# A fused attention, soft-MoE and FFN kernel: dispatch softmax by token tile, a ninth weight tile beside the streamed ones, and another order at the beginning

## The chip, the cores and the metric

The kernel runs on one core of one Trainium2 chip. The metric is the device time of one execution in microseconds (us). PE is TensorE (PEld its weight loads), DVE is VectorE, ACT is ScalarE, POOL is GpSimd, and SP issues most DMAs.

## The reference, cut to what matters

```python
# attention: B, H, S, D = 4, 8, 768, 64, a few global keys and a local window
scores = 0.125 * q @ k.T + bias             # masked
x = softmax(scores, -1) @ v                 # -> (3072 tokens, 512)
# soft MoE: 8 experts, 4 slots each = 32 slots
logits = x @ phi                            # (3072, 32)
d = exp(logits - logits.max(0)); d /= d.sum(0) + 1e-9   # dispatch: softmax over the tokens
slot_input = d.T @ x                        # (32, 512)
slot_out[e] = relu(slot_input[e] @ w1[e]) @ w2[e]       # w1 512x1024, w2 1024x512, float32
c = softmax(logits, 1); x = c @ slot_out    # combine: softmax over the slots
# second FFN
out = relu(x @ w_in) ** 2 @ w_out
```

## The kernel before, in words

Every engine has a queue of its own, and the kernel writes the order of all queues by hand; semaphores only make an engine wait. Three stages follow each other.

**Attention, to 184 us.** The work is 48 units (4 batches, 3 pairs of token tiles, 4 pairs of heads), two to an iteration of the loop at L538. A unit's steps are `stage_qk` (PE, scores `s`, L224), `stage_max` (DVE, mask and row maximum, L238), `stage_exp` (ACT, L257), `stage_T` (PE, transposes into `pt`, L268), `stage_ev` (copies to `pT`, L274, one on DVE and one on ACT), `stage_pv` (PE, `o`, L285) and `stage_x` (ACT, `xT`). Before the loop stands a hand-written beginning, with dummy matmuls (`warm`, L81) between the first steps, and the eight masks are built by DVE, ACT (mask 1, L159) and POOL (masks 2 to 7, L161).

Four units finish a chunk of 256 tokens, 12 chunks in all. A chunk goes through `route(k)`, a generator that is run in small steps (`step(n)`) between the stages of later units. Its front makes the logits: `lt` (L354), `pl` (L364), then on DVE `rc`, two products `lh` (L387) and a sum into `c_tok` (L343), then `px` (L333) and `xb` (L336). An odd chunk ends there; an even chunk goes on with its back, for itself and the odd chunk before (T = 4 token tiles of 128). The back is an online softmax over tokens with the 32 slots held four times over 128 partitions: POOL copies each logit four times (`l`, L391), PE transposes T blocks of 128x128 into `pq` (L406), DVE takes the maximum (L425), ACT the exponential (L427) and the correction factor `fo` (L428), PE transposes T blocks back into `pd` (L437), and `pS` (L455) adds to the running sum `acc`, each group of 32 partitions for another token tile, all with one maximum `nm`. Temporary PSUM tiles share four banks (tag "m"), so a transpose also waits until an earlier tile in its bank was read.

**Experts, 184 to 236 us.** 16 weight tiles of 2 MB (`w1_e`, `w2_e`) pass through SBUF. `NPRE` = 8 of them, the `w1`, have places of their own (`p0` to `p7`) and are loaded in 32 quarters during the loop. Three more places (`s0` to `s2`) come free with the attention's memory. All further loads go into places whose tile is used up, in the order of `items` with the places of `SLOTS` (L189), and the first FFN weights (`win_0`, `wout_0`, 1 MB each) stand ahead of `w2_7`, which comes in four parts. PE multiplies `w1` (L648, 16 matmuls a tile) and `w2` (L740). In program order DVE does `spread` (L717), then `conv_in(0)` and most of `conv_out(0)` (L750, L751, L754: the raw words of the FFN weights made float32), then the copy `soT` (L911), on which the FFN's first matmuls rest.

**FFN, 236 us to the end.** Two chained matmuls over five slices of the hidden width; nothing of it is changed but the places of two tiles.

Of the kernel before, what the change touches and what calls it, by code (L numbers as in the profile page):

```python
# [20 lines left out]
P = 128  # L21
# [7 lines left out]
EPS = 1e-9  # L29
NPRE = 8  # L30
TB = 256
WIDTHS = [256, 384, 512, 512, 384]
NBLK = NT // TB

C_ID, C_SI, C_SI4, C_R2, C_J = 0, 128, 160, 288, 416
C_W = 544
W_REL = S + (QT - 1) * P
# [3 lines left out]
def attention_moe_ffn(ctx: ExitStack, tc, qk, vx, nn, phi, w1, w2, w_in, w_out, consts, relw, out):  # L41
# [11 lines left out]
    ident = con[:, C_ID : C_ID + P]  # L53
    si = con[:, C_SI : C_SI + NS]
    si4 = con[:, C_SI4 : C_SI4 + P]
    n_i = full("n_i", [1, 4], I32)
    n_1 = full("n_1", [1, 4])
    n_f = full("n_f", [P, 4])
    phi_s = full("phi_s", [P, NPR, NS])
    phib = full("phib", [P, NPR, 2, NS])  # L60
# [74 lines left out]
    V.tensor_copy(n_1, n_i)  # L135
    warm(8, zero, idle)
    n_p = aps.tile([P, 512], F32, tag="m", name="n_p", bufs=4)
# [50 lines left out]
    wt = {}  # L188
    SLOTS = [f"p{i}" for i in range(NPRE)] + ["s0", "s1", "s2"] + [f"p{i}" for i in (0, 1, 4, 5, 6, 6, 7)]  # L189

# [123 lines left out]
    fronts = []  # L314

    def route(k, tail=False, back=True):
        xT = xTs[k]
        lg = c_tok[:, 2 * k : 2 * k + 2, :]
# [26 lines left out]
        if tail:  # L345
            ph = pl.rearrange("p (t h s) -> p t h s", h=H, s=NS)
            products(pl, range(2))
            yield
        else:
            pt = [bank(f"lt{k}_{hh}") for hh in range(2)]  # L350
            for pr in range(NPR):
                for hh in range(2):
                    r = slice(hh * D, hh * D + D)
                    nc.tensor.matmul(pt[hh][pr * NS : pr * NS + NS, 0:TB], lhsT=phi_s[r, pr, :], rhs=xT[r, pr, :], start=True, stop=True)  # L354
            yield
            lt = post.tile([P, 2, TB], F32, tag="lh", name=f"lt{k}")
# [14 lines left out]
        if tail:  # L371
            l5 = post.tile([P, 2, 5, NS], F32, tag="l5", name=f"l5{k}")
            scaled(lh[:, :, 0:4, :], 0, 4)
            added(l5[:, :, 0, :], lh[:, :, 0:4, :])
            xTs.pop(k)
            pl = bank(f"pl{k}_2")
            ph = pl.rearrange("p (t h s) -> p t h s", h=H, s=NS)
            products(pl, range(2, 4))
            yield
            scaled(l5[:, :, 1:5, :], 4, 8)  # L380
            added(lg, l5)
            yield
            turn(0, range(NPR))
            yield
        else:
            for t in range(2):
                V.tensor_tensor(lh[:, t].rearrange("p (h g) s -> p h g s", g=2), ph[:, t],  # L387
                                rc[:, t].rearrange("p (h g) -> p h g", g=2).unsqueeze(3).broadcast_to([P, NPR, 2, NS]), op=ALU.mult)
            added(lg, lh)
            l2 = post.tile([P, 2, 4, NS], F32, tag="l5", name=f"l2{k}") if back else att.tile([P, 2, 4, NS], F32, tag="l2", name=f"l2{k}", bufs=1)  # L390
            G.tensor_copy(l2, lg.unsqueeze(2).broadcast_to([P, 2, 4, NS]))  # L391
            for t in range(2):
                px.append(bank(f"px{k}_{t}"))
                turn(t, range(NPR))
                yield
                rows(t)
# [6 lines left out]
        pq = bank(f"pq{k}", tail)  # L403
        for t in range(T):
            if not tail:
                nc.tensor.transpose(pq[:, t * P : t * P + P], parts[t // 2][0][:, t % 2, :, :].rearrange("p a s -> p (a s)"), ident)  # L406
                continue
            for g in range(4):
                nc.tensor.matmul(pq[g * NS : g * NS + NS, t * P : t * P + P], lhsT=lg[:, t, :], rhs=ident, start=True, stop=True)
# [96 lines left out]
    for i in range(2):  # L506
# [13 lines left out]
        stage_max(i + 2, 1)  # L520
        if i == 1:

            G.memset(phib, 0.0)
            for hh in range(2):
                G.tensor_copy(phib[hh * D : hh * D + D, :, hh, :], phi_s[hh * D : hh * D + D, :, :])
        load_qk(i + 6)
# [517 lines left out]
def layout(inputs):  # L1044
# [34 lines left out]
    con[i, C_ID + i] = 1  # L1079
    con[i, C_SI + i % NS] = 1  # L1080
# [36 lines left out]
```

## Time and profile before

| | us |
|---|---|
| three runs | 539.74, 540.13, 541.6 (median 540.13) |
| the profiled execution, its own time | 541.12 |
| its span, first to last instruction | 539.2 |
| PE busy | 523.6 |
| DVE busy | 393.7 |
| ACT busy | 309.9 |
| POOL busy | 174.9 |

The span is 1.9 us shorter than the execution's own time. A busy share is an average over the three stages; what an engine limits is seen in a stage's own rows, in the idle time before an instruction (in brackets, with what ended it) and in the waits.

### The profile page before, as it was taken

The numbers are of one execution on the slowest core, as the hardware profiler recorded it, in microseconds if no ns is written. First come the engines' busy times: TensorE is split into PE (matmuls) and PEld (weight loads), VectorE is DVE, ScalarE is ACT, GpSimd is POOL, SyncE is SP. The second block draws the span as 40 slices with busy tenths as digits, with TensorE's granted clock in tenths as the row PEclk, the third lists the DMA queues.
The fourth block names the chain that finished last, engine by engine and source line by source line (L and its number), as shares of the span: only waits on it lengthen the run. The fifth ranks groups of instructions, "written<-read, shape, count | busy, mean of one in ns | idle before, by whom it ended". The sixth has DMA issues, their size and how long they took to land.

```text
span 539.2 us, 10211 instructions
## 1 busy us (share of the span) xinstructions
PE 523.6 (97%) x3659; PEld 394.9 (73%) x3659; DVE 393.7 (73%) x984; ACT 309.9 (57%) x813; POOL 174.9 (32%) x160
## 2 busy tenths in 40 slices
PE   8999999999999899899999999999999999999997
PEld 5786677777767734256778788878888878888885
DVE  5888879798888764558869897978857757545553
ACT  4987887878786511255775655545544445434441
POOL 7100000000000010024664576455554437544441
PEclk9999999999999999999999999999999999999999
DMA  8889999899962499953041304030030000003333
GB/s 263 271 265 325 322 321 303 312 330 313 325 200 79 161 422 424 416 221 131 27 157 19 139 1 157 0 118 0 1 117 1 0 2 1 0 2 117 118 117 117
DMA packets 25545, 89.13 MB, mean 165 GB/s; under 512 B 2834, under 2 KB 3474, under 8 KB 23314
## 3 DMA queue, kind: packets, MB, share of 16 engines
q1 hardware_dynamic: 25344, 88.30, 45.5%
q8 instruction: 30, 0.49, 0.4%
q14 instruction: 25, 0.20, 0.1%
q10 hardware_dynamic: 146, 0.13, 0.1%
HBM read 82.13 MB, written 6.29 MB: 164 GB/s over the span
## 4 chain that ended last, share of the span: by engine, by line
PE 74%; DVE 12%; DMA 6%; ACT 5%; issue 1%; POOL 1%; DVEq 0%; ACTq 0%; POOLq 0%
PE acc L859 14%; PE acc L860 14%; PE acc L861 14%; PE s L224 6%; PE pt L268 6%; DMA w<-in_w 6%; PE o L285 5%; PE h L841 3%; ACT sm L257 2%; DVE sm L238 2%; PE lt L354 1%; PE px L333 1%; DVE cvyi L751 1%; PE idle L81 1%; DVE rg L846 1%
## 5 line engine op out<-in xcount | busy, mean ns | idle before, releaser
L849 POOL TENSOR_TENSOR g<-rg,g 128x512 fp32r<-128x512 f32 (+1 forms) x109 | 136.8, 1257 | 166.1 <-DVE rg L846 163.4
L859 PE MATMUL acc<-w,g 128*128 128x512 f32 x384 | 151.8, 395 | 1.0 <-DVE oacc L865 1.0
L861 PE MATMUL acc<-w,g 128*128 128x512 f32 x384 | 150.2, 391 | 0.7 <-POOL g L849 0.7
L860 PE MATMUL acc<-w,g 128*128 128x512 f32 x384 | 150.7, 392 | 0.0
L845 ACT ACTIVATE rg<-h 128x512 f32<-128x512 f32 (+1 forms) x109 | 59.7, 548 | 122.0 <-PE h L841 110.8
L867 DVE TENSOR_TENSOR oacc<-acc,oacc 128x512 f32<-128x512 f32 x95 | 65.3, 687 | 58.3 <-PE acc L861 58.3
L257 ACT ACTIVATE sm<-sm,nm 128x256 f32<-128x256 f32 (+1 forms) x192 | 92.7, 486 | 12.3 <-DVE nm L244 10.9
L861 PEld LDWEIGHTS acc<-w,g 128*128 128x128 f32 x384 | 72.1, 188 | 18.6 <-POOL g L849 3.0
L859 PEld LDWEIGHTS acc<-w,g 128*128 128x128 f32 x384 | 72.1, 188 | 17.8 <-DVE oacc L865 1.8
L860 PEld LDWEIGHTS acc<-w,g 128*128 128x128 f32 x384 | 72.4, 189 | 11.1
L846 DVE SCALAR_TENSOR_TENSOR rg<-h,rg 128x512 f32<-128x512 f32 (+1 forms) x109 | 67.7, 621 | 17.1 <-ACT rg L845 17.1
L238 DVE CUSTOM_DVE_ANT_0 sm<-s,mask 128x256 f32<-128x256 f32 (+1 forms) x192 | 67.3, 396 | 4.0 <-PE s L224 3.1
L848 ACT ACTIVATE g<-rg 128x512 fp32r<-128x512 f32 (+1 forms) x109 | 63.4, 581 | 3.5
L391 POOL COPY l<-c_tok 128x256 f32<-128x256 f32 x11 | 4.4, 402 | 162.2 <-DVE c_tok L343 133.8
L224 PE MATMUL s<-raw 64*128 64x256 f32 (+1 forms) x384 | 52.6, 394 | 0.0
L268 PE MATMUL pt<-con,sm 128*128 128x128 f32 x352 | 46.4, 278 | 1.4 <-DVE xb L336 1.4
L285 PEld LDWEIGHTS o<-pT,v 128*64 128x64 f32 x704 | 37.9, 137 | 9.9 <-ACT pT L274 5.2
L285 PE MATMUL o<-pT,v 128*64 128x128 f32 x704 | 44.2, 276 | 0.5 <-issue 0.2
L268 PEld LDWEIGHTS pt<-con,sm 128*128 128x128 f32 x352 | 38.2, 141 | 7.8 <-DVE xb L336 2.9
L841 PEld LDWEIGHTS h<-cu 128*128 128x128 f32 x192 | 35.9, 188 | 7.3
L224 PEld LDWEIGHTS s<-raw 64*128 64x128 f32 x384 | 31.2, 191 | 12.5 <-issue 8.5
L841 PE MATMUL h<-cu 128*128 128x256 f32 x192 | 39.9, 280 | 0.0
(157 smaller groups left out, 567.9 us busy)
## 6 DMA issues: line engine op xcount, KB each, us to landing
raw<-in_qk SPq DMA_DIRECT2D x48, 384.0 KB, 5.6
w<-in_w SPq DMA_DIRECT2D x36, 512.0 KB, 6.8
w<-in_w SPq DMA_DIRECT2D x7, 2048.0 KB, 12.0
v<-in_vx SPq DMA_DIRECT2D x48, 256.0 KB, 4.2
out_x<-oacc SPq DMA_DIRECT2D x23, 256.0 KB, 2.0
win<-in_w_in SPq DMA_DIRECT2D x2, 2048.0 KB, 8.6
wout<-in_w_out SPq DMA_DIRECT2D x2, 2048.0 KB, 8.4
win<-in_w_in SPq DMA_DIRECT2D x2, 1536.0 KB, 10.4
```

The lines of the kernel that those rows point to most:

```text
L224: nc.tensor.matmul(sc[hh][:, tt, 0:n, :], lhsT=r[r0 : r0 + D, tt, :], rhs=rhs, start=True, stop=True)
L238: V.tensor_tensor_reduce(out=sm[:, j, 0:n, :], in0=sc[hh][:, tt, 0:n, :], in1=m[:, 2:3, :] if n == 1 else m[:, 0:2, :], scale=1.0, scalar= ...
L257: nc.scalar.activation(sm[:, j, 0:n, :], sm[:, j, 0:n, :], AF.Exp, bias=nm[:, j : j + 1], scale=QK_SCALE, accum_out=chunk_sums(i // NPR)[: ...
L268: nc.tensor.transpose(pp[tt][:, hh, c, :], sm[:, 2 * tt + hh, c, :], ident)
L285: nc.tensor.matmul(o[hh * D : hh * D + D, tt, :], lhsT=v[:, tt + 2 * c, hh * D : hh * D + D], rhs=pT[:, 2 * tt + hh, c, :], start=c == 0, ...
L841: nc.tensor.matmul(ph[:, k, :], lhsT=U[:, c0 : c0 + P], rhs=cst[:, n * TB : n * TB + TB], start=True, stop=True)
L846: V.scalar_tensor_tensor(g, ph[:, k0:k1, :], 0.0, r, op0=ALU.max, op1=ALU.mult)
L849: G.tensor_tensor(g2[:, 1, js, :], g, g2[:, 0, js, :].bitcast(F32), op=ALU.subtract)
L859: nc.tensor.matmul(pa, lhsT=ghi[:, j, ms], rhs=whi[:, j, :], start=j == 0, stop=False)
L860: nc.tensor.matmul(pa, lhsT=ghi[:, j, ms], rhs=wlo[:, j, :], start=False, stop=False)
L861: nc.tensor.matmul(pa, lhsT=glo[:, j, ms], rhs=whi[:, j, :], start=False, stop=j == J - 1)
L867: V.tensor_tensor(o, pa, o, op=ALU.add)
```

## The change

1. Chunks 0 to 8 (`UNITED` = 8) run the back's softmax apart for each token tile: the logits of up to four tiles are transposed at once, 128 tokens by up to 4 x 32 columns, so that each group of 32 partitions is one token tile with a maximum, a sum and a factor of its own. POOL's fourfold copy falls away, and one `yield` with it. After chunk 8, `unite()` takes the minimum of the four `nm`, rescales `rden` and `acc`, and adds up `rden` over the groups. Chunks 9 to 11 go as before.
2. `NPRE` is 9: `w2_0` gets a place `p8` and is loaded by four more quarters in two later iterations. `SLOTS` has one entry less behind the three streamed places. Room comes from constants (`si` is a part of `si4`, `phi_s` and its GpSimd copies into `phib` fall away, since the host lays out `phib`), from `soT` in a later pool and from a smaller reserved region for dynamic DMAs.
3. At the beginning a small Exp stands on ACT ahead of mask 1, so that its function table is loaded there, and `stage_qk(1)` follows `stage_qk(0)` with no dummy matmuls between; ten dummies instead of eight stand first, and six fall away.

```diff
-NPRE = 8
+NPRE = 9
-C_ID, C_SI, C_SI4, C_R2, C_J = 0, 128, 160, 288, 416
+C_ID, C_SI4, C_R2, C_J = 0, 128, 256, 384
-    phi_s = full("phi_s", [P, NPR, NS])
-    soT = full("soT", [P, 4, NS])
     nc.scalar.dma_start(n_i, nn)
+    nc.scalar.activation(rm[:, 0:1], zero[:, 0:1], AF.Exp)
-    warm(8, zero, idle)
+    warm(10, zero, idle)
-    SLOTS = [f"p{i}" for i in range(NPRE)] + ["s0", "s1", "s2"] + [f"p{i}" for i in (0, 1, 4, 5, 6, 6, 7)]
+    SLOTS = [f"p{i}" for i in range(NPRE)] + ["s0", "s1", "s2"] + [f"p{i}" for i in (0, 1, 4, 5, 5, 6)]
+    UNITED = 8
+    def unite():
+        old = run["nm"]
+        pn = bank("pn")
+        nc.tensor.transpose(pn[0:1, 0:P], old, ident)
+        m1 = post.tile([1, 4, NS], F32, tag="db", name="m1")
+        V.tensor_reduce(m1, pn[0:1, 0:P].rearrange("p (g s) -> p s g", s=NS).unsqueeze(1).broadcast_to([1, 4, NS, 4]), axis=AX.X, op=ALU.min)
+        yield
+        pm = bank("pm")
+        nc.tensor.matmul(pm[:, 0:1], lhsT=m1.rearrange("p g s -> p (g s)"), rhs=si[0:1, 0:1], start=True, stop=True)
...
+        V.tensor_copy(nm, pm[:, 0:1])
+        fo = post.tile([P, 1], F32, tag="fo", name="fou")
+        nc.scalar.activation(fo, old, AF.Exp, bias=nm, scale=-1.0)
+        V.tensor_tensor(rden, rden, fo, op=ALU.mult)
+        yield
+        pr = bank("pr")
+        nc.tensor.matmul(pr[:, 0:1], lhsT=si4, rhs=rden, start=True, stop=True)
+        V.tensor_copy(rden, pr[:, 0:1])
+        G.tensor_scalar(acc, acc, fo, None, op0=ALU.mult)
     def route(k, tail=False, back=True):
+        apart = k <= UNITED
...
-            l2 = post.tile([P, 2, 4, NS], F32, tag="l5", name=f"l2{k}") if back else att.tile([P, 2, 4, NS], F32, tag="l2", name=f"l2{k}", bufs=1)
-            G.tensor_copy(l2, lg.unsqueeze(2).broadcast_to([P, 2, 4, NS]))
+            l2 = None
+            if not apart:
...
+        R = slice(0, T * NS if apart else P)
+        C = P if apart else T * P
+        if apart:
+            nc.tensor.transpose(pq[R, 0:P], c_tok[:, 2 * k + 2 - T : 2 * k + 2, :].rearrange("p t s -> p (t s)"), ident)
+        for t in range(0 if apart else T):
...
-        V.tensor_reduce(mx[R], pq[R, 0 : T * P], axis=AX.X, op=ALU.max)
+        V.tensor_reduce(mx[R], pq[R, 0:C], axis=AX.X, op=ALU.max)
...
             yield
-            yield
+            if not apart:
+                yield
         pd = bank(f"pd{k}")
-        for t in range(T):
+        if apart:
+            nc.tensor.transpose(pd[:, R], dT[R, 0:P], ident[R, R])
+        for t in range(0 if apart else T):
...
+            if k == UNITED:
+                yield from unite()
...
-                    nc.tensor.matmul(pt[hh][pr * NS : pr * NS + NS, 0:TB], lhsT=phi_s[r, pr, :], rhs=xT[r, pr, :], start=True, stop=True)
+                    nc.tensor.matmul(pt[hh][pr * NS : pr * NS + NS, 0:TB], lhsT=phib[r, pr, hh, :], rhs=xT[r, pr, :], start=True, stop=True)
-    warm(6, zero, idle)
     stage_qk(0)
-    nc.sync.dma_start(phi_s, phi)
+    stage_qk(1)
+    nc.sync.dma_start(phib, phi)
...
     warm(5, zero, idle)
-    stage_qk(1)
     stage_max(0, 0)
```

In PE's queue, at the back of chunk 6 (its `pq` starts at 123.97 us in the trace of before), stand before the change `pq`, `stage_pv` of two units, `stage_qk` of one, and `pd`:

```order
L406 MATMUL pq_2019<-con,l_1782 128x128 x2
L406 MATMUL pq_2019<-con,l_1958 128x128 x2
L285 MATMUL o_2024<-pT_1981,v_1831 64x128 x8
L285 MATMUL o_2033<-pT_1992,v_1833 64x128 x8
L224 MATMUL s_0_2059<-raw_1941 128x256
L224 MATMUL s_1_2060<-raw_1941 128x256
L224 MATMUL s_0_2059<-raw_1941 128x256
L224 MATMUL s_1_2060<-raw_1941 128x256
L437 MATMUL pd_2079<-con,dT_2049 128x32 x4
L268 MATMUL pt_0_2084<-con,sm_1926 128x128 x4
```

and after it:

```order
L432 MATMUL pq_1984<-con,c_tok 128x128
L284 MATMUL o_1986<-pT_1946,v_1799 64x128 x8
L284 MATMUL o_1995<-pT_1957,v_1801 64x128 x8
L223 MATMUL s_0_2021<-raw_1908 128x256
L223 MATMUL s_1_2022<-raw_1908 128x256
L223 MATMUL s_0_2021<-raw_1908 128x256
L223 MATMUL s_1_2022<-raw_1908 128x256
L468 MATMUL pd_2041<-con,dT_2011 128x128
L267 MATMUL pt_0_2046<-con,sm_1893 128x128 x4
```

`pq` and `pd` are one transpose each instead of four, at the same places; `pS` comes one step earlier (ahead of the next unit's scores), and so does the whole front of the odd chunk that follows.

In DVE's queue, at the front of chunk 7, an odd one (the row ahead of these is the last row maximum of a unit; `pl` and `px` are PSUM tiles of PE), stand before:

```order
L244 TENSOR_SCALAR nm_2232<-mx_2231 128x4
L368 TENSOR_SCALAR rc_2161<-sums_1757 128x16
L369 RECIPROCAL rc_2161<-rc_2161 128x16
L387 TENSOR_TENSOR lh_2256<-pl_2202,rc_2161 128x256 x2
L343 TENSOR_REDUCE c_tok<-lh_2256 128x64
L336 TENSOR_TENSOR xb_2162<-px_0_2262,rc_2161 128x512
```

and after the change:

```order
L243 TENSOR_SCALAR nm_2137<-mx_2136 128x4
L391 TENSOR_SCALAR rc_2098<-sums_1737 128x16
L392 RECIPROCAL rc_2098<-rc_2098 128x16
L410 TENSOR_TENSOR lh_2168<-pl_2161,rc_2098 128x256 x2
L366 TENSOR_REDUCE c_tok<-lh_2168 128x64
L273 COPY pT_2187<-pt_0_2177 128x512
```

The products and their sum now stand ahead of the next iteration's copy `pT`, where before they stood behind that iteration's copies and maxima; `xb` of both tiles follows later, in one place.

SP's queue, from the loads of unit 45 on to the start of the experts (`w_7` is `w1_7`; of before, `w_0` to `w_2` are `w2_0` to `w2_2`):

```order
L103 DMA raw_2532<-in_qk 128x768
L103 DMA raw_2534<-in_qk 128x768
L109 DMA v_2536<-in_vx 128x512
L109 DMA v_2538<-in_vx 128x512
L103 DMA raw_2649<-in_qk 128x768
L109 DMA v_2651<-in_vx 128x512
L109 DMA v_2653<-in_vx 128x512
L109 DMA v_2765<-in_vx 128x512
L109 DMA v_2767<-in_vx 128x512
L205 DMA w_0_2978<-in_w 128x4096
L205 DMA w_1_2980<-in_w 128x4096
L205 DMA w_2_2982<-in_w 128x4096
```

and after the change (`w_0` is `w2_0`, now in quarters; `w_1` on are `w2_1` on):

```order
L204 DMA w_0_2380<-in_w 128x1024 x2
L102 DMA raw_2487<-in_qk 128x768
L102 DMA raw_2489<-in_qk 128x768
L108 DMA v_2491<-in_vx 128x512
L108 DMA v_2493<-in_vx 128x512
L204 DMA w_0_2380<-in_w 128x1024 x2
L102 DMA raw_2602<-in_qk 128x768
L108 DMA v_2604<-in_vx 128x512
L108 DMA v_2606<-in_vx 128x512
L108 DMA v_2728<-in_vx 128x512
L108 DMA v_2730<-in_vx 128x512
L204 DMA w_1_2947<-in_w 128x4096
```

Two pairs of quarters have come in between the last loads of the attention, and one load of 2 MB less remains behind it.

## Rows read from the trace of the kernel before

**Rows 1.** Chain that ended last, 184 to 240 us: start, us, what.
```profile
198.01 12.89 DMA w<-in_w
...
210.92 19.85 DMA w<-in_w
...
230.81 1.05 PE pSO L740 x4
...
233.67 0.30 DVE soT L911
```

**Rows 2.** DMA view, 180 to 235 us: throughput in 40 equal slices.
```profile
GB/s 0 0 214 334 465 405 429 405 453 417 447 405 453 375 453 393 399 441 441 405 411 441 441 417 405 441 441 411 393 417 405 426 390 405 417 432 429 429 429 429
```

**Rows 3.** Timeline, 184 to 240 us: start, us, engine, line, [idle before].
```profile
220.52 5.36 PE L740 MATMUL pSO<-w,hZ 128*32 128x512 f32 x48
220.81 1.04 DVE L717 TENSOR_TENSOR cu<-pc,cu 64x384 fp32r<-64x384 f32 x2 [1.62 <-ACT cu L716]
...
223.22 0.43 DVE L750 TENSOR_SCALAR cvyi<-raw 128x512 int32<-128x512 int32 x1 [1.37 <-DMA raw<-in_w_in]
...
231.43 0.69 DVE L754 SCALAR_TENSOR_TENSOR cvyo<-cvxo,cvyo 128x512 int32<-128x512 int32 x1
...
233.67 0.29 DVE L911 COPY soT<-pst 128x128 f32<-128x128 f32 x1 [1.55 <-PE pst L910]
```

**Rows 4.** Windows: stretch, its us, busy us of PE, PEld, DVE, ACT, POOL.
```profile
66.59:82.00 15.41, 15.00 (x166) 11.05 (x162) 11.64 (x44) 12.76 (x46) 0.03 (x1) 1.00 0.92 318
...
110.78:126.94 16.16, 15.90 (x166) 12.13 (x166) 15.55 (x60) 11.87 (x43) 0.81 (x2) 1.00 0.93 323
...
148.00:162.50 14.50, 14.07 (x136) 10.41 (x137) 12.53 (x49) 11.86 (x43) 0.40 (x1) 1.00 0.61 191
```

**Rows 5.** Waits, 16 to 184 us: engine, line, whom, total us, times, longest.
```profile
PEld pt L268 <- DVE xb L336: 2.9, 7, 0.8
...
PE pd L437 <- ACT dT L427: 1.4, 4, 0.4
PE pt L268 <- DVE xb L336: 1.4, 4, 0.6
```

**Rows 6.** Timeline of PE, 118 to 150 us.
```profile
123.97 0.66 PE L406 MATMUL pq<-con,l 128*128 128x128 f32 x4
124.55 1.97 PE L285 MATMUL o<-pT,v 128*64 128x128 f32 x32
...
127.78 0.43 PE L437 MATMUL pd<-con,dT 32*128 32x32 f32 x4 [0.19 <-ACT dT L427]
128.14 1.97 PE L268 MATMUL pt<-con,sm 128*128 128x128 f32 x16
...
143.90 0.66 PE L268 MATMUL pt<-con,sm 128*128 128x128 f32 x4 [0.26 <-DVE xb L336]
```

**Rows 7.** Timeline of DVE, 118 to 150 us.
```profile
124.94 0.68 DVE L425 TENSOR_REDUCE rmax<-pq 128x1 f32<-128x512 f32 x1
```

**Rows 8.** Timeline, 0 to 16 us.
```profile
5.58 1.65 PE L224 MATMUL s<-raw 64*128 64x128 f32 x8
...
5.86 1.28 ACT L159 ACT_TABLE_LOAD   x1 [5.86 <-DVE mtmp L147]
...
6.11 7.24 POOL L161 TENSOR_SCALAR mask<-mtmp 128x384 bf16<-128x384 f32 x6
...
7.27 0.29 DVE L238 CUSTOM_DVE_ANT_0 sm<-s,mask 128x128 f32<-128x128 f32 x1 [0.85 <-PE s L224]
...
10.48 0.93 PE L224 MATMUL s<-raw 64*128 64x128 f32 x8
...
12.24 0.59 ACT L274 COPY pT<-pt 128x512 f32<-128x512 f32 x1 [0.44 <-PE pt L268]
```

**Rows 9.** Windows, as rows 4; the granted clock follows POOL.
```profile
4.00:5.60 1.60, 1.60 (x10) 0.92 (x9) 1.20 (x5) 0.00 (x0) 0.96 (x3) 1.00 1.00 293
...
15.00:20.00 5.00, 5.00 (x48) 3.62 (x44) 4.14 (x23) 5.00 (x20) 0.07 (x2) 1.00 0.97 318
```

More of the change, by code (lines that the diff above doesn't have):

```diff
@@ L33 @@
 NBLK = NT // TB
-C_ID, C_SI, C_SI4, C_R2, C_J = 0, 128, 160, 288, 416
-C_W = 544
+C_ID, C_SI4, C_R2, C_J = 0, 128, 256, 384
+C_W = 512
 W_REL = S + (QT - 1) * P
@@ L53, in attention_moe_ffn @@
     ident = con[:, C_ID : C_ID + P]
-    si = con[:, C_SI : C_SI + NS]
     si4 = con[:, C_SI4 : C_SI4 + P]
+    si = si4[:, 0:NS]
     n_i = full("n_i", [1, 4], I32)
@@ L314, in attention_moe_ffn @@
     fronts = []
+    UNITED = 8
[8 more added lines that the diff above has]
+        nc.tensor.matmul(pm[:, 0:1], lhsT=m1.rearrange("p g s -> p (g s)"), rhs=si[0:1, 0:1], start=True, stop=True)
+        nm = post.tile([P, 1], F32, tag="nmr", name="nmu", bufs=2)
+        run["nm"] = nm
+        V.tensor_copy(nm, pm[:, 0:1])
[7 more added lines that the diff above has]
+        G.tensor_scalar(acc, acc, fo, None, op0=ALU.mult)
     def route(k, tail=False, back=True):
+        apart = k <= UNITED
         xT = xTs[k]
@@ L389, in route @@
             added(lg, lh)
-            l2 = post.tile([P, 2, 4, NS], F32, tag="l5", name=f"l2{k}") if back else att.tile([P, 2, 4, NS], F32, tag="l2", name=f"l2{k}", bufs=1)
-            G.tensor_copy(l2, lg.unsqueeze(2).broadcast_to([P, 2, 4, NS]))
+            l2 = None
+            if not apart:
+                l2 = post.tile([P, 2, 4, NS], F32, tag="l5", name=f"l2{k}") if back else att.tile([P, 2, 4, NS], F32, tag="l2", name=f"l2{k}", bufs=1)
+                G.tensor_copy(l2, lg.unsqueeze(2).broadcast_to([P, 2, 4, NS]))
             for t in range(2):
@@ L415, in route @@
         yield
-        R = slice(0, P)
         old = run["nm"]
@@ L424, in route @@
         dT = post.tile([P, 2 * TB], F32, tag="dT", name=f"dT{k}")
-        V.tensor_reduce(mx[R], pq[R, 0 : T * P], axis=AX.X, op=ALU.max)
+        V.tensor_reduce(mx[R], pq[R, 0:C], axis=AX.X, op=ALU.max)
         V.scalar_tensor_tensor(nm[R], mx[R], -1.0, old[R], op0=ALU.mult, op1=ALU.min)
-        nc.scalar.activation(dT[R, 0 : T * P], pq[R, 0 : T * P], AF.Exp, bias=nm[R], scale=1.0, accum_out=dn[R])
+        if apart and T == 2:
+            V.tensor_copy(nm[2 * NS : P], old[2 * NS : P])
+        nc.scalar.activation(dT[R, 0:C], pq[R, 0:C], AF.Exp, bias=nm[R], scale=1.0, accum_out=dn[R])
         nc.scalar.activation(fo[R], old[R], AF.Exp, bias=nm[R], scale=-1.0)
@@ L433, in route @@
             yield
-            yield
+            if not apart:
+                yield
         pd = bank(f"pd{k}")
-        for t in range(T):
+        if apart:
+            nc.tensor.transpose(pd[:, R], dT[R, 0:P], ident[R, R])
+        for t in range(0 if apart else T):
             nc.tensor.transpose(pd[:, t * NS : t * NS + NS], dT[0:NS, t * P : t * P + P], ident[0:NS, 0:NS])
@@ L472, in route @@
             V.scalar_tensor_tensor(acc[A], acc[A], fo[A], pS[A], op0=ALU.mult, op1=ALU.add)
-            if T == 2 and k:
+            if T == 2 and not apart:
                 A = slice(2 * NS, P)
                 V.tensor_scalar(acc[A], acc[A], fo[A], None, op0=ALU.mult)
+            if k == UNITED:
+                yield from unite()
     queue = []
@@ L520, in attention_moe_ffn @@
         stage_max(i + 2, 1)
[L521 to L525, printed above, removed]
         load_qk(i + 6)
@@ L692, in attention_moe_ffn @@
         G.memset(odd[r0 : r0 + NS], -1.0)
+    soT = ex.tile([P, 4, NS], F32, tag="soT", name="soT")
     crs = {}
@@ L1079, in layout @@
     con[i, C_ID + i] = 1
-    con[i, C_SI + i % NS] = 1
     for g in range(4):
@@ L1085, in layout @@
     relw = (i[:, None] - np.arange(W_REL)[None, :] + (QT - 1) * P).astype(np.float32)
+    phi = pm(inputs["moe_phi"], 4)
+    phib = np.zeros((P, 4, 2, NS), phi.dtype)
+    for hh in range(2):
+        phib[hh * D : hh * D + D, :, hh, :] = phi[hh * D : hh * D + D].reshape(D, 4, NS)
     w1, w2 = inputs["moe_w1"], inputs["moe_w2"]
@@ L1090, in layout @@
         "nn": words([np.asarray(inputs[n], np.int64) for n in ("n_local", "n_global")]).reshape(1, 2).view(np.int32),
-        "phi": pm(inputs["moe_phi"], 4),
+        "phi": phib,
         "w1": np.ascontiguousarray(w1.reshape(E, 4, P, F).transpose(0, 2, 1, 3)),
@@ L1103 @@
     from concourse.bass_utils import run_bass_kernel_spmd
-    nc = bacc.Bacc("TRN2", target_bir_lowering=False, num_devices=1)
+    nc = bacc.Bacc("TRN2", target_bir_lowering=False, num_devices=1, dynamic_dma_scratch_size=1024)
     lay = layout(inputs)
```

## The prediction

> **What bounds the kernel now.** I read the chain of work that ended last first, because it shows which stage is held by something else than PE. It names PE nearly everywhere, but between 198.01 and 230.77 us two pieces of a DMA of weights hold it [rows 1]. The DMA view of that stretch says why: from about 185 us on it moves 375 to 465 GB/s in every slice without a gap [rows 2]. So the experts' stage is as long as its 18 MB take (eight tiles of `w2` and two of 1 MB), and the last 2 MB tile, which comes in four parts, decides: PE has finished the tile before at 225.88 (220.52 and 5.36), but the matmuls of the fourth part start only when it has landed, at 230.81, and end at 231.86 (1.05 more) [rows 1, 3].
>
> The attention is different. Its windows (after the stretch: length, busy time with the count of instructions of each engine, granted clock, DMA share, GB/s) show PE busy 15.90 of 16.16 us where an even chunk's back runs, and 15.00 of 15.41 where an odd front runs [rows 4]. PE's only waits of size there are 1.4 us for the exponential ahead of `pd` and 1.4 us for DVE's `xb` ahead of a transpose, whose weight loads wait 2.9 us [rows 5]. So PE time that is saved in an even back should be gained, as long as DVE, busy 15.55 of the 16.16 us, follows.
>
> In the beginning DVE's first maximum waits for PE's scores, at 7.27 us, and the masks are late too: ACT's table load starts only at 5.86 and takes 1.28 us ahead of mask 1 [rows 8].
>
> **The change part by part.** *Ninth tile, loads.* `w2_0` (2.097 million bytes) leaves the full stretch. At 430 GB/s, the middle of rows 2, that is 4.9 us: every later load lands 4.9 us sooner. Its four quarters go into two later iterations. The stretch 148.0 to 162.5 moves 191 GB/s at a share of 0.61, and 2.1 MB in 14.5 us more are 145 GB/s, together 336, beside 318 and 323 in the stretches before [rows 4]. The only queue that they pass is SP's, whose next loads wait for PE anyway; I take nothing for it. Without that cover two quarters would delay the next scores' data by 2.4 us (1.05 MB at 430 GB/s).
>
> *What is late next.* PE would finish the last tile at 225.88 and a third of 5.36 (16 of 48 matmuls, 1.79), 227.67 instead of 231.86: 4.2 us. But the copy `soT` at 233.67 stands on DVE behind the conversion, which began at 223.22 because the raw words landed then, and ended at 232.12 (231.43 and 0.69), 8.90 us later [rows 3]. With the words 4.9 us sooner it begins when DVE is done with `spread`, at 221.85 (220.81 and 1.04), and ends at 230.75. `soT` then stands there, 2.9 us sooner, not 4.2. I take **-2.9**, bounds -1.4 (only the conversion's shift) and -4.2.
>
> *Even backs.* Four transposes of `pq` hold PE from 123.97 to 124.55, 0.145 each, four of `pd` from 127.78 to 128.14 [rows 6]. One each remains: 0.58 + 0.36 - 2 x 0.145 = 0.65, in four backs with T = 4 (chunks 2, 4, 6, 8) 2.6, and 0.2 in chunk 0 with T = 2. The wait ahead of `pd` (1.4 in four) goes as well: the maximum over 512 columns takes 0.68 [rows 7], over 128 an estimate of a quarter to a half of that, and the exponential shrinks too, while `pd` keeps its place behind the same PE work. Together **-4.2**; bounds 0, if another engine binds, and -4.2. The copies of POOL hide beside others and are worth nothing alone.
>
> *Odd fronts.* One `yield` less brings each odd front forward by a step. DVE forms `lh` and `c_tok` in a gap where it waited for transposes, and `xb` is done before the transposes that need its bank. The 1.4 us that PE waited for `xb` go: **-1.4**. Upper bound the 2.9 of the weight loads, lower nothing: the copy `pT` is now behind those products, and `stage_pv` waits for it.
>
> *`unite`.* Three small transposes or matmuls on PE, at most 0.145 each: **+0.4**. Worse could be DVE: its copy of `nm` waits for `pm`, which stands on PE behind two units of `stage_pv` (1.97 from first to last [rows 6]). Behind that copy on DVE wait the next unit's maxima, then its exponential, then its transposes, an iteration later. PE has those two units, scores and four transposes queued meanwhile, so I charge no more; the bound is +2.
>
> *Beginning.* With the table loaded early, mask 1 no longer waits 1.28 us, and with no dummies between, both units' scores are done sooner. The first maximum can start when mask 0 is there, about 0.7 us before 7.27. Behind the copy at 12.24 ACT is the engine without a gap (5.00 of 5.00 us from 15 to 20 [rows 9]), so what it starts earlier is what the stage gains: **-0.7**, bounds 0 and -1.3. More is not to be had, since POOL's last mask ends at 13.35 (6.11 and 7.24) [rows 8].
>
> Sum: -2.9 - 4.2 - 1.4 + 0.4 - 0.7 = -8.8. The profiled execution took 541.12 us, so 532.3; the median of the runs, 540.13, lies 1.0 below that execution, so **531.3**. The FFN stage only shifts.
>
> **The rivals.** *DVE takes over in the attention* (0.20). For it: 15.55 of 16.16 us busy in an even back [rows 4], and in `unite` it stands still. Then an even back gains only what DVE sheds, an estimated 0.4 (0.68 less a good third) each, 1.6, odd fronts nothing, and `unite` costs its 2: the attention loses 0.4; with 0.7 and 2.9 the gain is 3.2: 536.9. Against it: in the odd stretch DVE has 3.8 us free of 15.41.
>
> *The experts' stage does not gain* (0.07): the ninth tile is resident, but a load waits for its place, or the conversion holds the same time. The sum without 2.9 is 5.9: 534.2.
>
> *More is gained* (0.10): 4.2 in the experts (1.3 more), 2.9 in the odd fronts (1.5 more), 1.3 at the beginning (0.6 more). All three make 12.2 and 527.9, two of them about 10.9 and 529.
>
> *Nothing measurable* (0.03): the attention goes as in the first rival (0.4 lost), and the conversion does not move; of the beginning's 0.7 then 0.3 remains, 539.8.
>
> *Slower, by PE's clock at the beginning* (0.03). [...]
>
> **How the numbers follow.** The forecast has 0.57, its own range 529.5 to 533.5 (odd fronts and `unite` at either bound). From 528.0 to 537.0 the first three rivals are in; nothing and slower lie out, and what the others spill over: about 0.1. Within 0.3% (1.6 us) a measurement of this kernel can't tell a change from none. Faster by more: 0.57 + 0.20 + 0.07 + 0.10 = 0.94, of which I take 0.01 away for mishaps; same 0.03; slower 0.04.
>
> **What the profile of the changed kernel would show.** The chain should hold PE, ACT or DVE at `soT`, no longer a DMA up to it, and the conversion should begin right behind `spread`. `pq` and `pd` should be one matmul each, with no wait for the exponential, and the wait of transposes for `xb` be gone. About 5 us should lie between the old and the new end of the attention (184 us), of them 0.7 by the copy that stood at 12.24. Around `unite` DVE should show an idle time of 1 to 2 us for `pm` that PE does not follow. I am wrong if PE waits for DVE's `pT` in odd chunks or for `pm` and `pr`, if scores wait for their data near 150 us, or if the conversion is later than DVE allows.

## The result, and the profile after

The changed kernel takes 532.16 us (median of four runs, 532.12 to 532.35) against 540.42 for the kernel before (539.74 to 541.6): a ratio of 0.9846, with a 95% interval from 0.9828 to 0.9864. The profiled execution took 532.15 us with a span of 530.1. Three positions divide the gain of 9.1 us in the span: the copy `slotZ`, which ends the attention, moved from 193.97 to 188.16 (5.81); from there to the copy `soT` it is 36.85 us instead of 39.70 (2.85); what follows took 0.44 less.

The chain of work that ended last, 176 to 240 us (start, us, what), holds no DMA any more up to `soT`, where [rows 1] had 32.74 us of it:

```profile
206.03 5.29 PE pSO L770 x48
...
216.07 0.44 DVE cvyi L780
...
224.28 0.69 DVE cvyo L784
225.01 0.30 DVE soT L941
```

The conversion begins right behind `spread`, without a wait, and `soT` follows its last operation at once: from 215.01 to 225.30 DVE pauses for 0.68 us only, for ACT. In the attention, the windows over the same two stretches of iterations as the first two of [rows 4] (columns as there):

```profile
65.27:80.03 14.76, 14.47 (x161) 10.97 (x161) 12.74 (x47) 11.10 (x40) 0.00 (x0) 1.00 0.93 315
107.80:122.25 14.45, 14.45 (x159) 11.40 (x159) 13.38 (x55) 11.87 (x43) 0.00 (x0) 1.00 0.95 332
```

In the stretch with an even back PE is now busy all the time. The lengths can't be compared as they stand, since these windows begin and end at loads that SP issues: the second one of the kernel before still holds both `xb` of the odd front ahead of it, which the change has brought forward out of the window. In the back itself DVE sheds 0.40 us, by its maximum (0.68 in [rows 7], 0.28 now). The timeline of DVE before, and then after:

```profile
110.84 0.67 DVE L336 TENSOR_TENSOR xb<-px,rc 128x512 f32<-128x512 f32 x1
...
113.00 0.68 DVE L336 TENSOR_TENSOR xb<-px,rc 128x512 f32<-128x512 f32 x1
```

```profile
105.86 1.28 DVE L359 TENSOR_TENSOR xb<-px,rc 128x512 f32<-128x512 f32 x2
...
120.58 0.28 DVE L453 TENSOR_REDUCE rmax<-pq 128x1 f32<-128x128 f32 x1
```

Between the same two steps of PE, the scores of one unit and those of the fourth unit behind it (110.88 to 126.45 before, 107.31 to 121.76 after), it is 15.57 us and 14.45: 1.12 less. The waits of 16 to 180 us, beside [rows 5]:

```profile
PEld pd L468 <- ACT dT L457: 2.3, 5, 0.5
...
PEld pt L267 <- ACT pT L273: 2.2, 4, 0.7
...
DVE nmu L328 <- PE pm L325: 1.5, 1, 1.5
...
PE pt L267 <- ACT pT L273: 1.3, 4, 0.4
...
PEld pt L267 <- DVE xb L359: 1.1, 2, 0.8
...
PE pt L267 <- DVE xb L359: 0.6, 1, 0.6
```

The waits for `xb` shrank, from 2.9 and 1.4 to 1.1 and 0.6, but transposes now wait 1.3 us for ACT's `pT`; the weight loads ahead of `pd` still wait 2.3 of 3.4 us for the exponential. PE's timeline beside [rows 6] has `pq` and `pd` of chunk 6 as one matmul each, and `pd` shows no wait:

```profile
119.60 0.33 PE L432 MATMUL pq<-con,c_tok 128*128 128x128 f32 x1
...
119.86 1.97 PE L284 MATMUL o<-pT,v 128*64 128x128 f32 x32
...
122.84 0.33 PE L468 MATMUL pd<-con,dT 128*128 128x128 f32 x1
...
123.01 1.91 PE L267 MATMUL pt<-con,sm 128*128 128x128 f32 x16
```

Up to the start of what follows, these two hold PE for 0.26 and 0.17 us, where the four of each in [rows 6] held it for 0.58 and 0.36.

And the beginning, beside [rows 8]:

```profile
1.32 1.28 ACT L85 ACT_TABLE_LOAD   x1 [1.32 <-PEq L1138]
...
5.09 2.93 PE L223 MATMUL s<-raw 64*128 64x128 f32 x16 [0.79 <-DMA raw<-in_qk]
...
6.15 7.24 POOL L160 TENSOR_SCALAR mask<-mtmp 128x384 bf16<-128x384 f32 x6
6.77 0.29 DVE L237 CUSTOM_DVE_ANT_0 sm<-s,mask 128x128 f32<-128x128 f32 x1 [0.32 <-PE s L223]
...
7.95 1.35 PE L79 MATMUL idle<-zero 128*128 128x256 bf16 x9
```

ACT's copy `pT` that stood at 12.24 now starts at 11.00, and `pq` of chunk 0 at 33.28 instead of 34.44: 1.16 us sooner.

### The profile page after: what moved, and what is told of

Same layout as the page of the kernel before. It is cut to its first block, busy times and chain, and to the rows that moved or that the text cites. A ratio compares the mean times of both kernels' runs of the same rounds, so it can differ in the third digit from the quotient of the medians.

```text
span 530.1 us, 10143 instructions
## 1 busy us (share of the span) xinstructions
PE 515.7 (97%) x3634; PEld 393.2 (74%) x3634; DVE 392.5 (74%) x989; ACT 308.0 (58%) x815; POOL 170.2 (32%) x149
## 4 chain that ended last, share of the span: by engine, by line
PE 50%; DVE 9%; ACT 1%; issue 1%; POOL 1%; DVEq 0%; POOLq 0%
PE acc L889 14%; PE acc L890 14%; PE acc L891 14%; PE h L871 3%; DVE cvyi L781 1%; DVE rg L876 1%; PE pSO L770 1%; DVE cvyi L780 1%; DVE cvyo L781 1%; DVE oacc L895 1%; PE pre L677 1%; DVE cvyo L780 1%; PE pu L830 1%; DVE winf L784 1%; DVE oacc L897 1%
## 5 line engine op out<-in xcount | busy, mean ns | idle before, releaser
L879 POOL TENSOR_TENSOR g<-rg,g 128x512 fp32r<-128x512 f32 (+1 forms) x109 | 135.2, 1243 | 164.8 <-DVE rg L876 132.8
L336 POOL TENSOR_SCALAR acc<-acc,fou 128x512 f32<-128x512 f32 x1 | 1.6, 1568 | 143.9 <-ACT fou L330 143.9
```

Source lines behind the costliest of these rows:

```text
L879: G.tensor_tensor(g2[:, 1, js, :], g, g2[:, 0, js, :].bitcast(F32), op=ALU.subtract)
```

## The experiments

Each kernel below is the changed one with the edit shown, timed against the kernel before (540.13 to 540.42 in these comparisons). The table gives the places from which the attention is read: the start of `pq` in chunks 0 and 8 and of the copy `slotZ`, and the distances between them.

| kernel | time | pq 0 | pq 8 | slotZ | pq 0 to 8 | pq 8 to slotZ |
|---|---|---|---|---|---|---|
| before | 540.42 | 34.44 | 153.26 | 193.97 | 118.82 | 40.71 |
| changed | 532.16 | 33.28 | 147.74 | 188.16 | 114.46 | 40.42 |
| e2, joint softmax | 538.58 | 33.70 | 152.57 | 193.28 | 118.87 | 40.71 |
| e5, late step | 537.94 | 34.24 | 150.38 | 193.16 | 116.14 | 42.78 |
| e10, late step but in 8 | 536.25 | 33.75 | 149.93 | 190.35 | 116.18 | 40.42 |
| e6, no uniting | 533.53 | 33.31 | 147.77 | 187.60 | 114.46 | 39.83 |
| e7, PE padded | 537.17 | 33.30 | 149.76 | 190.80 | 116.46 | 41.04 |

**e1: the ninth tile undone.**

```diff
-NPRE = 9
+NPRE = 8
-    ... for i in (0, 1, 4, 5, 5, 6)]
+    ... for i in (0, 1, 4, 5, 6, 6, 7)]
```

> The changed kernel with only the ninth tile undone (eight tiles ahead, w2_0 streamed again). Theory: the experts' stage loses what the prediction gave it, 2.9 us, so 535.0 us; the first fourth of the last w2 tile waits for its DMA again, and the attention ends where it ended with the tile, near 188.2 us. Rival, PE alone decides and DVE's conversion does not: 4.2 us, 536.4. Rival, the ninth tile is worth nothing because the rest of the stage is as long: 532.2.

536.69 us (536.17 to 537.38; ratio 0.9933, 0.992 to 0.9946): 4.5 lost, more than either theory. `slotZ` stands at 188.25, but `soT` 41.34 us behind it, 1.64 more than in the kernel before. PE's timeline and a window show where:

```profile
222.51 1.05 PE L770 MATMUL pSO<-w,hZ 128*32 128x512 f32 x4 [2.17 <-DMA w<-in_w]
223.79 4.00 PE L770 MATMUL pSO<-w,hZ 128*32 128x512 f32 x12 [0.23 <-DMA w<-in_w]
```

```profile
222.50:228.00 5.50, 5.26 (x19) 0.97 (x20) 4.17 (x8) 1.36 (x3) 0.00 (x0) 0.69 1.03 430
```

Most of it is a later landing. The first part of the last tile came 34.26 us behind `slotZ`, not 33.03 as before (227.00), and the raw words of the FFN weights 30.48 us behind it (218.73), not 29.25. The DMAs were issued at the same distances to 0.2 us, and why they landed 1.2 us later stays open. The other 0.4 is PE's: behind its wait for the tile (2.17 us) the granted clock averaged 0.69 from 222.5 to 228 us, where the kernel before shows 1.00 throughout from 210 to 243, and from the first of these products to the end of the last it took 5.28 us instead of 4.86. The times of the five runs don't follow the clock: those with a mean granted clock of 1.000 took 536.17, 537.08 and 537.38 us, those with 0.996 took 536.46 and 536.69.

**e2: the joint softmax back.**

```diff
-    UNITED = 8
+    UNITED = -1
-            if T == 2 and not apart:
+            if T == 2 and k:
```

> The changed kernel with only the dispatch softmax undone (joint over the groups in all chunks, POOL's fourfold copy and the second yield back, no uniting). Theory: PE time and PE waits come back, 4.2 for the even backs and 1.4 for the odd fronts less 0.4 for the uniting, 5.2 us by the prediction and 4.6 by the two traces, so 536.8 to 537.4. Rival, DVE bounds the attention and the change gained only what DVE sheds there: 1.6 at most, 532.2 to 533.8.

538.58 us (536.68 to 538.77; 0.9958, 0.9946 to 0.9971), 6.4 lost. `slotZ` is 5.12 later, as the theory says, 0.42 of it by the beginning and 4.70 by the chunks; DVE is not the bound. The experts take 36.84 us, as in the changed kernel. Another 1.6 lie behind `soT` in the trace (an execution of 538.72 us): the first FFN product starts 5.03 us after it instead of 3.39, because the granted clock averaged 0.60 from 231 to 234 us. One of the six runs, of which there is no trace, took 536.68. e9 and e12 look at this.

**e3: the beginning undone.**

```diff
-    nc.scalar.activation(rm[:, 0:1], zero[:, 0:1], AF.Exp)
-    warm(10, zero, idle)
+    warm(8, zero, idle)
+    warm(6, zero, idle)
     stage_qk(0)
-    stage_qk(1)
...
     warm(5, zero, idle)
+    stage_qk(1)
```

> The changed kernel with only the beginning undone (eight dummies, six more ahead of the first scores, five between the two units' scores, no early Exp). Theory by the two traces: ACT's copy that stood at 12.24 and now at 11.00 goes back and all behind it follows, 1.2 us, 533.4. The prediction's size would give 0.7, 532.9. Rival, what is gained there is lost again before the loop has run some rounds: 532.2. [...]

533.02 us (0.987, 0.9856 to 0.9885), 0.9 lost, and `slotZ` at 189.14, 0.98 later. What the beginning gains is carried to the end.

**e8: only the early Exp undone.**

```diff
-    nc.scalar.activation(rm[:, 0:1], zero[:, 0:1], AF.Exp)
```

> The changed kernel without the early Exp on ACT, so that its table is loaded ahead of mask 1 again, while the order of the scores and dummies stays the new one. Theory: the table load is what made mask 1 late, and most of the gain at the beginning (0.9 us by the undone beginning) is its: 532.9 to 533.1, the second copy pT of unit 0 back near 12.0 us from 11.00. Rival, the gain is that of the earlier scores: 532.2 to 532.4, the copy near 11.0 to 11.3.

The timeline of this kernel shows the table load late again, DVE waiting for mask 1, and then the same wait for one of POOL's masks at the same time as in the changed kernel (13.43 there):

```profile
5.92 1.28 ACT L157 ACT_TABLE_LOAD   x1 [5.92 <-DVE mtmp L145]
...
7.77 0.29 DVE L236 CUSTOM_DVE_ANT_0 sm<-s,mask 128x128 f32<-128x128 f32 x1 [0.85 <-ACT mask L157]
...
13.44 0.29 DVE L236 CUSTOM_DVE_ANT_0 sm<-s,mask 128x128 f32<-128x128 f32 x1 [0.48 <-POOL mask L159]
```

`slotZ` stands at 188.20. So in the trace the early table load is worth nothing: POOL's masks, which end near 13.4 us, hold the beginning either way, and the gain is that of the earlier scores, the rival. Other traces agree: in those of e4, e6 and e11, which have the early load, ACT's copy `pT` starts at 10.18 to 10.28 us, here at 10.95, and `pq` of chunk 0 at 33.30 to 33.40, here at 33.29. The times are less clear: 532.85 us median (531.98 to 532.99), and the profiled execution is the one with 531.98. Whether the others lost 0.7 at the beginning can't be read.

**e5 and e10: the second yield back, in all backs run apart, or in all but that of chunk 8.**

```diff
-            if not apart:
+            if not apart or k < UNITED:
                 yield
         pd = bank(f"pd{k}")
```

(e5 has the `yield` without a condition.)

> The changed kernel, but the even backs of the chunks run apart keep their second yield, so that pd, pS and all of the odd front behind them come a step later, as before the change. Theory: the step brought the odd fronts forward and that alone is worth 1.4 us, so 533.6, with the end of the attention (the copy slotZ, 188.16 us in the changed kernel) near 189.6. Rival, the step only traded PE's wait for xb against its new wait for ACT's pT (1.3 us in four): 532.2, slotZ near 188.2. Rival, the later step is better: 531, and then it belongs into a best version.

> The changed kernel with the second yield back in the backs of chunks 0, 2, 4 and 6, but not in chunk 8, so that the uniting stands at the places of the changed kernel. Of the 5.0 us by which the late step in all backs moved the end of the attention, the trace puts 1.7 between the backs of chunks 0 and 8, 2.0 behind the back of chunk 8, and 1.0 ahead of the first. Theory: the odd fronts are worth 1.4 to 1.7 us and the 2.0 belong to the uniting at its later places: slotZ near 189.9, 533.9. Rival, the odd fronts are worth 3.5 us or more by themselves: slotZ at 191.5 or later, 535.7 or more.

e5 took 537.94 us (0.9951, 0.9938 to 0.9964), e10 536.25 (0.9919, 0.9904 to 0.9934). e5's 5.8 looked as if the odd fronts were the whole change. The table takes it apart. From `pq` 0 to `pq` 8 both kernels lose the same, 1.7 us against the changed one: that is the odd fronts, as the theory has it. Behind `pq` 8, e5 loses 2.36 more and e10 nothing: in e5 the uniting stands a step later, and PE's `pr` waits 1.6 us for DVE there, which the changed kernel doesn't show (waits, 16 to 184 us, of e5):

```profile
ACT fou L330 <- DVE nmu L328: 1.9, 1, 1.9
...
PE pr L334 <- DVE rden L331: 1.6, 1, 1.6
```

The odd front of chunk 9 stands a step later with the uniting; its share of the 2.36, 0.3 to 0.6 us by the other four, is not told apart.

Ahead of `pq` 0, e5 lost 0.96 and e10 0.47, though nothing of their edit has run by then: there PE's nine dummies took 2.10 us in both, against 1.35 in the changed kernel (last section). The rest of e10's 4.1 is 0.5 between `slotZ` and `soT` (e5 has it too), and 1.5 behind `soT`, as in e2 (granted clock 0.65 and 0.78 from 228 to 234 us).

**e6: no uniting.**

```diff
-            if k == UNITED:
+            if k == UNITED and False:
```

> The changed kernel with the uniting left out; from chunk 8 on the four groups keep maxima of their own, so the sum over the slots' tokens is not that of the reference, and only the time is read. Theory: uniting costs PE three small operations, 0.4 us, and DVE's idle times for it are covered, so 531.8 with slotZ near 187.8. Rival, DVE's idle time for pm (1.5 us) reaches PE an iteration later: 530.2 to 530.7, slotZ near 186.4.

`slotZ` comes 0.56 us sooner, at 187.60, all of it behind `pq` 8 (39.83 against 40.42): the theory. The time is nevertheless longer, 533.53 us (532.36 to 535.49): in the trace 0.4 us is lost between `slotZ` and `soT` and 1.6 behind `soT`, where the granted clock fell here too (0.71 and 0.72 from 225 to 231 us). By its time alone this run would have said the opposite of what it shows.

**e7: PE's old count of transposes.**

```diff
             nc.tensor.transpose(pd[:, R], dT[R, 0:P], ident[R, R])
+            for t in range(1, T):
+                nc.tensor.transpose(pd[:, 2 * P : 2 * P + P], con[:, 0:P], ident)
```

(and the same for `pq`.)

> The changed kernel with the matmul count of before in the backs run apart: three more transposes of a constant beside each pq and each pd in chunks 2, 4, 6 and 8 (one more each in chunk 0), into columns that nobody reads. Nothing else is added, so this is PE's share of the even backs by itself. Theory, PE bounds the attention there: 26 transposes of 0.145 us are 3.8 us, slotZ near 191.9 and the time near 536. Rival, DVE or ACT bound it and PE has the time: 532.2 to 533.

`slotZ` is 2.64 us later (537.17 us, 0.9938, 0.9923 to 0.9954). Every added transpose lengthens the attention, by 0.10 us each: PE bounds it, and the rival is out. The size that I gave was too large, since a further transpose behind others adds less than 0.145. Nor is 2.64 the price of the old transposes: those added beside `pd` are 128 columns wide where the old ones were 32, so that `pq` and `pd` of chunk 6 hold PE for 0.58 and 0.49 us here, for 0.58 and 0.36 in the kernel before. The rest of the 5.0 us by which the time grew is not the edit's: 1.4 lie between `slotZ` and `soT`, where PE's weight loads pause for 1.1 us at 205 us and nothing in the trace says why, and 1.3 behind `soT`, as in e2 (granted clock 0.68 and 0.75 from 228 to 234 us).

**e4 and e11: `soT` ahead of the conversion's last part, and then the next loads out of the way.**

```diff
-            next(c1)
-            next(c1)
     SO = ex.tile([P, DM], F32, tag="e", name="SO", bufs=2)
     nc.scalar.copy(SO, pSO)
+    load_part(1, nc.scalar)
...
     V.tensor_copy(soT, ...)
-    for _ in c1:
-        pass
+    next(c1)
...
     next(u)
+    next(c1)
     next(u)
     warm(5, con, idle)
     next(u, None)
+    for _ in c1:
+        pass
```

(e4 is without the line `load_part(1, nc.scalar)`; in e11 the call on SP's queue falls away.)

> The changed kernel, but the conversion of the second half of the first output weights stands behind the copy soT instead of ahead of it, on DVE and ACT. Theory: after the ninth tile it is this conversion, not PE and not a DMA, on which soT waits (DVE has no gap from 216.07 to 225.01); without it the copy SO follows the last product at 222.2 at once and soT stands near 224.1, 0.9 us sooner, so 531.3. Rival, PE's own chain (pSO, SO, pst) already decides: no change, 532.2. Rival, the conversion is late for the first FFN products: 532.5 or more.

> The changed kernel with the conversion behind soT, as in the run that moved it, and the loads of the second FFN slice issued on ACT's queue behind the copy SO instead of on SP's during the last w2 tiles. Theory: with the conversion out of the way the last parts of w2_7 decide (its 64 products took 7.79 us where 7.07 were seen with no wait), and these two loads share the throughput with them; without them the products end 0.5 to 0.7 us sooner, 531.1 to 531.3. Rival, the parts of w2_7 are ahead of those loads anyway: 531.8. Rival, the second slice's data are late for its conversion at 231.3 us: 532.5 or more.

e4 took 531.76 us (531.25 to 532.09; ratio 0.984), e11 531.24 (530.94 to 533.58; 0.9848, 0.983 to 0.9866). The timelines of e4 and then e11:

```profile
214.98 7.79 PE L770 MATMUL pSO<-w,hZ 128*32 128x512 f32 x64
...
224.56 0.29 DVE L939 COPY soT<-pst 128x128 f32<-128x128 f32 x1 [1.18 <-PE pst L938]
```

```profile
214.74 7.07 PE L770 MATMUL pSO<-w,hZ 128*32 128x512 f32 x64
...
224.08 0.29 DVE L938 COPY soT<-pst 128x128 f32<-128x128 f32 x1 [0.93 <-PE pst L937]
```

`soT` waited for DVE before, and for PE's `pst` now: 225.01, 224.56, 224.08. So the conversion did decide, but with it gone only 0.45 us came, since the last products, held up by their DMA, took 7.79 us (7.43 in the changed kernel, 7.75 in e8); with the loads behind them they took 7.07 and the next 0.5 came. In the trace e11 beats the changed kernel by 0.9 us; in the runs its interval overlaps, so that e11 is the better of the two is shown of the place `soT`, not of the time.

**e9 and e12: the ninth tile alone, and with PE's pauses filled.** e9 is e2 and e3 together. e12 adds:

```diff
-    warm(7, con, idle)
+    warm(13, con, idle)
     pst = bps.tile([P, 512], F32, tag="sel", name="pst")
...
+    warm(6, con, idle)
     V.tensor_copy(soT, pst[:, : 4 * NS].rearrange("p (k s) -> p k s", s=NS))
```

> The kernel before with the ninth tile alone (joint softmax in all chunks and the old beginning). Theory of the prediction: soT follows DVE's conversion, 2.9 us sooner, so 537.5. Rival, the ninth tile is worth the 4.5 us that it cost to take it out of the changed kernel: 535.9. [...]

e12 rests on e9's trace: there PE paused for 0.84 us ahead of `pst` and 0.78 us ahead of `pu`, and its granted clock then averaged 0.54 from 231 to 234 us and 0.89 from 234 to 237. The added dummies stand in these two pauses.

> [...] Theory: the pauses made the clock fall, and without them soT stays at 36.85 us behind slotZ and the first products of the FFN follow it in 3.39 us instead of 4.87: 1.5 us less, 536.8, so that the ninth tile is worth the 2.9 to 3.5 us of the prediction by itself. Rival, the fall comes from something else there and stays: 538.3. Rival, the dummies stand in the way of pst and pu: 538.5 or more.

e9 took 538.26 us (536.71 to 539.08; 0.9961, 0.9946 to 0.9976), e12 537.56 (537.03 to 538.02; 0.9946, 0.9931 to 0.9961). In both, `soT` stands 36.85 and 36.86 us behind `slotZ`, 2.85 less than before. e9 then loses half of it. Its timeline of PE and its window of 230 to 234 us, and the same of e12:

```profile
229.08 1.08 PE L940 MATMUL pst<-con,SO 128*128 128x32 f32 x8 [0.84 <-ACT SO L935]
230.94 0.85 PE L830 MATMUL pu<-hZ,soT 128*32 128x256 f32 x8 [0.78 <-DVE soT L941]
231.72 1.25 PE L79 MATMUL idle<-con 128*128 128x256 bf16 x5
232.76 1.06 PE L845 MATMUL pu<-evu,con 128*128 128x256 f32 x2
```

```profile
230.00:234.00 4.00, 3.22 (x19) 1.79 (x19) 1.54 (x3) 1.13 (x3) 0.00 (x0) 0.65 0.36 154
```

```profile
228.83 1.08 PE L940 MATMUL pst<-con,SO 128*128 128x32 f32 x8 [0.19 <-ACT SO L935]
...
230.77 0.64 PE L830 MATMUL pu<-hZ,soT 128*32 128x256 f32 x8 [0.21 <-DVE soT L942]
231.34 0.72 PE L79 MATMUL idle<-con 128*128 128x256 bf16 x5
231.94 0.70 PE L845 MATMUL pu<-evu,con 128*128 128x256 f32 x2
```

```profile
230.00:234.00 4.00, 3.79 (x35) 2.63 (x33) 1.77 (x4) 1.36 (x3) 0.00 (x0) 1.00 0.31 132
```

With the pauses filled the clock stays at 1.00, and the first FFN product starts 3.47 us behind `soT` (233.81) instead of 4.87 (235.46). That is the mechanism of the theory. Of the 1.5 us expected, the two traces give 1.4 and the medians 0.7, with intervals that overlap. The mean granted clock was 0.997 in five of e9's runs, 0.998 in the sixth (536.71 us), and 0.998 to 1.000 in e12's.

## Why the prediction was right, step by step

The forecast was 531.3 us from the median, 532.3 against the profiled execution; the times are 532.16 and 532.15. The mechanisms of four of the five terms held, and the sum is off by 0.5 us, of 8.8 in the working and 8.3 in the medians. In part the errors cancel: the five terms measure -2.9, -3.5, -1.7, +0.6 and -1.2, less for the even backs against more for the odd fronts and the beginning.

- **Experts, -2.9: right, for the reason given.** 39.70 became 36.85, with the tile alone as well (e9, e12), and what is late next is DVE's conversion (e4). The upper bound of 4.2 was taken from PE alone. e4 shows that it could not have been had: once the conversion is away, the last DMA parts are there, 0.7 us later than PE. "I take nothing" for the four quarters' place held: PE's scores show no wait for their data near 150 us, their weight loads 1.4 us in three waits from 130 to 180 us (0.3 before).
- **Even backs, -4.2: right mechanism, too large; 3.5.** Between `pq` 0 and `pq` 8, the joint softmax takes 118.87 us and the late step 116.18, so backs alone gain 2.69 there: 0.85 for each of three (from `pq` 2 to `pq` 8: 89.32 in e2, 86.76 in e10), 0.13 for chunk 0. With a fourth of 0.85 for chunk 8 it is 3.5. Both parts of the term were sized too large. The transposes, 2.8 in the working, are 2.3: the one that remains holds PE for 0.26 and 0.17 us and not for 0.145, so a back of four saves 0.52, not 0.65. Of the wait ahead of `pd` I gave all 1.4 away, and some 1.1 came (from the end of `pq` to `pd` it is 0.25 to 0.32 us less in each of the four backs); the weight loads still wait 2.3 of 3.4 us for the exponential.
- **Odd fronts, -1.4: right, 1.7** (e10). PE's waits for `xb` went only partly and a new one for `pT` came, yet the four odd stretches gained 0.3 to 0.6 each, so adding up these waits would have missed it.
- **`unite`, +0.4: right, 0.6** (e6). DVE's idle time for `pm` is there, 1.53 us, and PE doesn't follow. That holds at this place in the order only: a step later it costs 2.4 more, the odd front behind it included (e5), which is the bound of 2 that I kept for it, by PE's wait for `rden` rather than through the maxima.
- **Beginning, -0.7: the size within its bounds (1.2 in the two traces, 0.9 by e3's time and 1.0 by its `slotZ`), one of its two reasons not borne out.** The step that failed is "With the table loaded early, mask 1 no longer waits 1.28 us". Mask 1 does come sooner, but in the trace of e8, where it doesn't, nothing is lost by the time POOL's last mask is made. The earlier scores carry the gain, up to that bound, which the prediction had named: over all traces `pq` 0 follows ACT's copy `pT` by 22.2 us where the copy starts at 11.50 us or later (seven traces), and stands at 33.28 to 33.40 where it starts at 11.00 or sooner, down to 10.18 (seven); in these DVE waits for POOL's mask at 13.43 to 13.54 us. That the changed kernel came down to the bound was in part luck (last section).

**The rivals.** DVE does not take over: in an even back it shed the 0.40 us that I allowed it, each back gained 0.85 all the same, and e7 shows PE as the bound. The 15.55 of 16.16 us from which this rival started held two `xb` of the odd front ahead (1.35 us). "Experts do not gain" and "nothing measurable" are out. "More is gained" came true in part only, in the odd fronts and the beginning. "Slower, by PE's clock at the beginning" did not happen: the most that any trace of the new order shows of it is the 0.96 us of e5 ahead of `pq` 0, where PE was slower while the granted clock read 1.00 (below). What no rival had is the clock's fall behind the experts (0.60 from 231 to 234 us in e2, 0.54 in e9). That the changed kernel escaped it (mean granted clock 0.998 to 1.000 in its four runs) was luck, as far as this forecast goes.

**Why the parts don't add up.** Undone one at a time, the ninth tile, the dispatch and the beginning cost 4.5, 6.4 and 0.9 us, 11.8 together, where all three gave 8.3. In e2 the fall of PE's clock is counted as well (0.60; 1.6 us), and in e1 the later landings (1.2 us) and a little of the clock (0.69; 0.4 us).

## What to carry to other kernels

Read an experiment at the place where its part ends (here `pq`, `slotZ` and `soT`) before reading its time: e6's time said the opposite of its trace, and e10's held 2.5 us that its edit had not made. Where a DMA is taken off the chain, look for what stands within half a microsecond behind it, since here the conversion, the last DMA and PE's products lay that close and each fix was worth only the distance to the next. Where work of an online step is reordered, the step at which its small dependent operations are issued can be worth as much as the work removed: one `yield` less gave 1.7 us in the odd fronts, and at its later place the uniting, with the front behind it, costs 2.4 more.

## What the runs showed of the hardware

**PE's clock behind two short pauses.** Ahead of `pst` and `pu` PE pauses for ACT and DVE. In e2, e7, e9 and e10 the pauses are 0.83 to 0.84 and 0.78 us, in e6 1.23 and 0.79, and in all five the granted clock fell behind them: taken in windows of 3 us it averaged 0.54 to 0.71 in the first, 0.72 to 0.89 in the second, and 1.00 from there to 243 us. The first FFN product came 1.3 to 1.6 us later behind `soT` than in the changed kernel. In the changed kernel, e3 and e5 they are 0.41 to 0.50 and 0.78 to 0.79, and it read 1.00 in every such window from 210 to 243 us, as with e12's 0.19 and 0.21. The changed kernel has the shorter first pause only because its last DMA parts hold PE up (7.43 us for the 64 products, against 7.07), so 0.36 us less of that wait would give it the 0.83 us of the others (an estimate); in e4 and e11 the pauses are shorter (at most 0.29 and 0.38 us), and the clock read 1.00. e9 and e12 differ in dummies alone, and their granted clocks were 0.65 and 1.00 from 230 to 234 us. At what length of pause the clock falls, and why, is not shown. A trace is of one execution; over the runs the mean granted clock goes with the time only in part. In e10 the one run with 1.000 took 534.55 us and the five with 0.995 to 0.997 took 535.44 to 536.62, but in e2 two runs with 1.000 took 536.68 and 538.77, the others 538.15 to 538.72.

**PE's durations at the beginning.** With the same order of work up to there, the nine dummies ahead of the third unit's scores took 1.35 us in the changed kernel (7.95 us, shown above), and in e5:

```profile
7.63 2.10 PE L79 MATMUL idle<-zero 128*128 128x256 bf16 x9
9.67 1.52 PE L223 MATMUL s<-raw 64*128 64x128 f32 x8
```

That is 0.23 us a dummy instead of 0.15, as with the first ten in both kernels (2.31 us from 1.47 on), and the eight scores behind took 1.52 us instead of 0.93. The granted clock reads 1.00 in both from 4.4 to 14 us, and why PE was slower in e5 is not shown. The execution was 0.96 us later at `pq` 0. With the new order, the copy `pT` starts at 10.18 to 11.00 us in the seven traces where the nine dummies took 1.16 to 1.76 us, and at 11.50 to 12.03 in the three where they took 2.10. Over all traces, `pq` 0 starts between 33.28 and 34.24 us with the new order (ten kernels, seven of them by 33.40) and between 33.88 and 34.44 with the old (four): some 0.9 us between the middles, with a spread as large, much of which goes with when PE's operations became shorter. How much the order is worth where that time is equal, two traces bound: in e2 (new) the nine dummies that end at 9.80 us still took 0.23 us each, in e3 (old) PE became faster a little sooner, within eight scores that end at 9.81 and took 1.50 us (1.65 for the eight before), and `pq` 0 stands at 33.70 and 34.24. So the order gives at least 0.5 (an estimate from these two), and the rest of the changed kernel's 1.2 goes with when PE became faster.
